# Chunk attention, gated projection and squared-ramp MLP on one core: heads swap rows by half block, weight combinations stored by pair into one tensor, a rounding step placed apart

## The chip, the cores and the metric

One core of one Trainium2 chip runs the whole program. The metric is the device time of one execution in microseconds (us); lower is better. All inputs and the output lie in the core's DRAM.

## The reference

Float64 inputs, q, k and v of 8 batches x 8 heads x 576 rows x 64, and five weight matrices. Attention works inside chunks of 64 rows; its output, 4608 tokens x 512, goes through a gated projection and then a second two-layer MLP. Cut to what matters:

```
scores = scale * matmul(q_c, k_c.T)            # per chunk of 64 rows, 9 chunks a head
attn = exp(scores - max); attn /= sum(attn) + 1e-9
x = matmul(attn, v_c)                          # (4608, 512) over the heads
x = (sigmoid(x @ w_gate) * (x @ w_val)) @ w_out        # d_ff 1536
h = x @ w2_in                                  # d_ff 2048
g = where(h >= 1, h, where(h <= -1, 0, (h + 1)**2 / 4))
out = g @ w2_out
```

q, k and v arrive as float32. The weights arrive as 8-byte floats, which the kernel itself turns into float32.

## The kernel before, in words

The program has four stages, one after the other.

**Stage 1** is attention and the gated projection, and it is the only one that the change touches. The 4608 tokens are cut into 9 blocks of 512 (`BS`), numbered 0 to 8. For each block, 24 projections (12 of w_gate, 12 of w_val, 12 matmuls each in `proj`: three products of high and low halves for each of 4 row groups) run on TensorE; ScalarE applies the sigmoid (L873), VectorE multiplies (L876), and the result is stored to DRAM (`g_store`, L760). One projection is one *slot*; a block is `NS` = 24 slots. Attention of block b is written into the slots of block b-1 (`later_block`), four head pairs `p` for each block: `load` brings q and k (L278), `v_load` brings v (L293), `t` transposes on VectorE (L304), `s` makes scores (L321), `m` and `e` subtract the maximum and take the exponential (L331 to L341), `n` and `w` normalise (L346 to L354), `p` and `c` transpose back (L360, L363), `o` multiplies with v (L373), `x` and `l` split the result into a high and a low half (L388, L392). Block 0's attention runs ahead of everything in `first_block`.

Because two 64-row heads share 128 partitions, the kernel gives the two heads turns at the upper and lower half: which head's chunk lies in which half of the rows flips ("trades") with every group `g` of 128 tokens, through the index `h ^ odd`. `v_load` therefore fetches v in pieces of at most two chunks, for each head apart.

In the same slots, from slot 26 on, the weights of the three later stages are made ready: `s_prep` takes a pair of weight tiles every 7 slots (22 pairs). It loads them (`w_load`), turns the 8-byte words into float32 (`w_low` and the VectorE half of `w_bits`, then a scaling on ScalarE, L124, then `w_join`), forms sums on GpSimd (`s_sums`), splits into high and low halves (`s_split`) and stores seven combinations (`s_spool`, L183) that the later stages load back (`s_load`, L187).

**Stages 2 to 4** (`down("o")`, `up`, `down("p")`) are matmuls with 7 products for 8 quarters, with operands from DRAM.

The order of the work is written out by hand: `at(slot, prio, fn, ...)` sorts the calls of a slot by fraction, priority and order of entry, and each engine does its share strictly in that order. All transfers are issued by SyncE (SP in the profile), one after the other. In the program's rows below, each transfer also waits for one of eight landing semaphores in turn (`DMAHW0` to `DMAHW7`), that is for the landing of the transfer eight before it.

Of the kernel before, what the change touches and what calls it, by code (L numbers as in the profile page):

```python
# [8 lines left out]
F32 = mybir.dt.float32  # L9
# [20 lines left out]
def kernel(  # L30
# [15 lines left out]
    nc = tc.nc  # L46
    P = 128
# [5 lines left out]
    CH = 64  # L53
    BS = 512
# [14 lines left out]
    dp = ctx.enter_context(tc.tile_pool(name="dp", bufs=1, space=bass.MemoryType.DRAM))  # L69
# [3 lines left out]
    uT = [dp.tile([F2 * P, GT], F32, name=f"uT{g}") for g in range(NG)]  # L73

    NWT = {"o": 7 * F1 // 4, "i": 7 * F2 // 4, "p": 7 * F2 // 4}
    sw = {
        kind: [dp.tile([P, 2, 2, 256], F32, name=f"sw{kind}{i}") for i in range(n)] for kind, n in NWT.items()
    }

    def f32(t):  # L80
        return t.bitcast(F32)
# [6 lines left out]
    keys = [(kind, f) for f in range(F1) for kind in "gv"]  # L88
    W = {}
    raws = {}  # L90
    stage = {}

    def words(raw):
        return lambda i, dt: raw.bitcast(dt).rearrange("p (n w) -> p n w", w=2)[:, :, i]
# [23 lines left out]
    def w_bits(key):  # L118
        word = words(raws[key])
        nc.vector.scalar_tensor_tensor(  # L120
            out=word(0, I32), in0=word(1, I32), scalar=-(2**31), in1=word(0, I32),
            op0=ALU.bitwise_and, op1=ALU.bitwise_or,
        )
        nc.scalar.activation(word(1, F32), word(1, F32), AF.Copy, scale=2.0**-112)  # L124

    def w_join(key):
# [28 lines left out]
    def s_place(kind, p, k):  # L155

        if kind == "i":
            return k // 2 * 7 + PO.index(p), k % 2
        return PO.index(p) * ((F1 if kind == "o" else F2) // 4) + k // 2, k % 2
# [18 lines left out]

    def s_spool(kind, k, part):
        products, st = stage.pop((kind, k, part))  # L180
        for i, p in enumerate(products):
            tile_, unit = s_place(kind, p, k)
            nc.sync.dma_start(out=sw[kind][tile_][:, unit], in_=f32(st[:, i]))  # L183

    def s_load(kind, i):
        w = wp.tile([P, 2, 2, 256], F32R, tag="w", name="w")
# [7 lines left out]
    def s_prep(kind, k):  # L194

        half_ = (F1 if kind == "o" else F2) // 2
        a, b = (kind, k), (kind, k + half_)
        return [
            (0, w_load, a), (0, w_load, b), (5, w_low, a), (5, w_bits, a), (6, w_low, b), (6, w_bits, b),
            (7, w_join, a), (7, w_join, b), (8, s_sums, kind, k), (9, s_split, kind, k, 0), (9, s_split, kind, k, 1),  # L200
            (10, s_split, kind, k, 2), (11, s_spool, kind, k, 0), (11, s_spool, kind, k, 1),
            (11, s_split, kind, k, 3), (12, s_spool, kind, k, 2), (13, s_spool, kind, k, 3),
        ]


# [3 lines left out]
    X = {}  # L209
# [24 lines left out]
    class Whole:  # L234
# [49 lines left out]
        def v_load(self, p):  # L284

            self.V[p] = t = self.alloc("vd").rearrange("p i (c e) -> p (i c) e", e=D)
            for off, m, bb, s0 in runs(self.b * BS, BS):
                c = off // CH
                while c < (off + m) // CH:
                    n = 2 - c % 2 if (off + m) // CH - c >= 2 else 1  # L290
                    for h in range(2):
                        at_ = s0 + c * CH - off
                        nc.sync.dma_start(  # L293
                            out=t[heads[h ^ c // 2 % 2], c:c + n],
                            in_=v[bb, 2 * p + h, at_:at_ + n * CH].rearrange("(c k) d -> k c d", k=CH),
                        )
                    c += n

        def t(self, p):
            qk, how, ident = self.qk[p], self.how[p], kv_["ident"]  # L300
# [25 lines left out]
        def m(self, p):  # L326
            s = self.SP[p][:, 0].rearrange("p (g h k) -> p g h k", h=2, k=CH)
            m = cp.tile([P, 2, NC], F32, tag="m0", name="m", bufs=2)
            banks = self.B.pop(("s", p))
            for h, b in enumerate(banks):  # L330
                nc.vector.tensor_reduce(out=m[:, h], in_=b, axis=AX.X, op=ALU.max)  # L331
            for h, b in enumerate(banks):
                for odd in range(2):
                    gs = slice(odd, NC, 2)
                    nc.vector.tensor_tensor(
                        out=s[:, gs, h ^ odd], in0=b[:, gs],
                        in1=m[:, h, gs].unsqueeze(2).to_broadcast([P, NC // 2, CH]), op=ALU.subtract,
                    )

# [25 lines left out]
        def o(self, p):  # L365

            banks = [self.bank(4 + r, [P, NC, 2, CH], "O") for r in range(2)]
            for g in range(0, NC, 2):
                for i in range(2):
                    for odd in range(2):  # L370
                        c = 2 * (g + odd) + i
                        for r, rows in enumerate(heads):
                            nc.tensor.matmul(  # L373
                                banks[r][heads[r ^ odd], g + odd, i],
                                lhsT=self.V[p][rows, c], rhs=self.SP[p][rows, 1, chunks[c]], start=True, stop=True,
                            )
            self.B["o", p] = banks

        def parts(self, p):
            for h, hs in enumerate(heads):  # L380
                for odd in range(2):
                    hi, lo = (X[self.b, p][hs, i].rearrange("p (g t) -> p g t", t=P)[:, odd::2] for i in range(2))
                    yield hi, lo, self.B["o", p][h ^ odd][hs, odd::2].rearrange("p g i t -> p g (i t)")

        def x(self, p):
            X[self.b, p] = x_tile()
# [7 lines left out]
    def first_block():  # L394
        ft = ps.tile([P, BS], F32, tag="b5", name="fill")

        def fill(n):
            for _ in range(n):
                nc.tensor.matmul(ft, lhsT=z[:, :P], rhs=z, start=True, stop=True)

        pieces = []
        for i in range(NW + 1):
            pieces.append((w_low, keys[i]))
            pieces.append((w_bits, keys[i]))
            if i:
                pieces.append((w_split, keys[i - 1]))
        nl = [0]

        def wl(n):
            for _ in range(n):  # L410
                w_load(keys[nl[0]])
                nl[0] += 1

        def conv(n):
            while n and pieces:
                fn, key = pieces.pop(0)
                fn(key)
                if fn is w_split and nl[0] < NW + 5:
                    wl(1)
                n -= fn is not w_low  # L420

        z = pool["sg"].tile([P, BS], F32R, tag="sg", name="z", bufs=4)
        nc.vector.memset(f32(z), 0.0)
        kv_["ident"] = cp.tile([P, P], F32, name="ident")
        make_identity(nc, kv_["ident"])
        a = Whole(
            0, [["b0", "b2", "b4"], "b1", "b3", "b6", "b7", "b5"],
            lambda nm: wp.tile([P, 2, BS], F32, tag="w", name=nm), "MVMT",
        )
        for c in LOADS:  # L430
            if c == "w":
                wl(1)
# [12 lines left out]
        conv(99)  # L445
        assert nl[0] == NW + 5, nl

# [39 lines left out]
    banks, B0, B1, OP, R_ = {}, {}, {}, {}, {}  # L487
# [280 lines left out]
    NW = 4  # L768
    for i, key in enumerate(keys):
        if i >= NW + 5:  # L770
            at(i - NW - 5, 2.5, w_load, key)
        if i > NW:
            at(i - NW - 1, 6, w_low, key)
            at(i - NW - 1, 6, w_bits, key)
        if i >= NW:
            at(i - NW, 5.5, w_split, key)
    slot = 26
    for kind, n in (("o", F1 // 2), ("i", F2 // 2), ("p", F2 // 2)):
        for pair in range(n):
            for dt, fn, *args in s_prep(kind, pair):  # L780
                at(slot + dt, 6 + dt / 10, fn, *args)
            slot += 7
# [11 lines left out]
    for i in range(FIRST):  # L794
        key, name = ("o", 0, i), ("o", 0, 1, i)
# [123 lines left out]
```

## Time and profile before

| | us |
|---|---|
| median of 3 runs | 1787.81 |
| the 3 runs | 1793.92, 1786.58, 1787.81 |
| the profiled execution | 1794.13 |
| its span in the trace | 1792.3 |
| its mean granted TensorE clock, share of full | 0.965 |

The trace gives busy time of the compute engines (PE is TensorE, PEld its weight load, DVE VectorE, ACT ScalarE, POOL GpSimd), waits with what ended them, the chain of work that ended last, and for SyncE the time in which each transfer was being issued (SPq) and when it landed. SyncE has no column of busy time; it is read from its timeline.

### The profile page before, as it was taken

Reading aid. Unit: us, or ns where it says so; the run is one execution under the profiler, and the core shown is the slowest. Engines: PE = TensorE matmul, PEld = TensorE weight load, DVE = VectorE, ACT = ScalarE, POOL = GpSimd, SP = SyncE. Lnnn points to the kernel's source line nnn. Section 1 sums busy time; section 2 is a strip of 40 time slices with the busy share of each in tenths; the row PEclk is TensorE's granted clock in tenths of the full one; section 3 lists DMA queues with packets and bytes.
Section 4 is the critical chain, followed back from the end, with each engine's and each line's share of the span. In section 5 each row is a group of like instructions: output and inputs, shape, how many; then the busy total and the mean of one; then the engine's idle time right before and its main releaser. Section 6 shows DMA issues by size and latency. Waiting matters only on the chain.

```text
span 1792.3 us, 30409 instructions
## 1 busy us (share of the span) xinstructions
PE 1677.1 (94%) x10658; PEld 1537.8 (86%) x10658; DVE 1193.9 (67%) x1874; ACT 870.0 (49%) x1632; POOL 833.7 (47%) x755
## 2 busy tenths in 40 slices
PE   6679987997889799999999999999999999999998
PEld 4567876776777678889999999999999989999998
DVE  5765544553545446217877787878887797889876
ACT  4554543443444255214555555555555445455453
POOL 2331442342334234106777775435442277677765
PEclk7889998998999899999999999999999999999999
DMA  6564565666666568683464465333234964644552
GB/s 159 142 174 114 161 199 171 169 195 177 180 180 199 170 168 241 219 302 106 154 223 142 142 235 223 142 147 144 106 142 182 360 228 123 169 143 105 133 150 36
DMA packets 392777, 307.19 MB, mean 171 GB/s; under 512 B 274992, under 2 KB 305712, under 8 KB 392624
## 3 DMA queue, kind: packets, MB, share of 16 engines
q1 hardware_dynamic: 392624, 305.24, 55.2%
q8 instruction: 84, 1.38, 0.3%
q14 instruction: 69, 0.57, 0.1%
HBM read 179.83 MB, written 125.30 MB: 170 GB/s over the span
## 4 chain that ended last, share of the span: by engine, by line
PE 63%; SPq 16%; DMA 9%; DVE 7%; issue 3%; ACT 1%; POOL 1%; DVEq 0%; ACTq 0%; POOLq 0%
PE P L471 16%; PE P L472 16%; PE P L470 16%; SPq L278 7%; SPq L293 5%; PE pr L470 5%; PE pr L471 4%; PE pr L472 4%; DMA gT<-sg 3%; DVE z L503 2%; DMA raw<-in_moe_w_gate_dram 2%; SPq L183 2%; DMA swi<-st 1%; DMA raw<-in_moe_w_out_dram 1%; DVE z L514 1%
## 5 line engine op out<-in xcount | busy, mean ns | idle before, releaser
L514 POOL TENSOR_TENSOR z<-z 128x384 fp32r<-128x384 f32 x305 | 356.3, 1190 | 308.7 <-ACT z L507 305.3
L471 PE MATMUL P<-z,w 128*128 128x384 f32 x1344 | 451.4, 336 | 4.9 <-POOL z L514 3.1
L470 PE MATMUL P<-z,w 128*128 128x384 f32 x1344 | 450.3, 335 | 0.0
L472 PE MATMUL P<-z,w 128*128 128x384 f32 x1344 | 450.1, 335 | 0.0
L470 PE MATMUL pr<-x,w 128*128 128x512 f32 x864 | 354.5, 410 | 0.0
L471 PE MATMUL pr<-x,w 128*128 128x512 f32 x864 | 345.7, 400 | 0.0
L472 PE MATMUL pr<-x,w 128*128 128x512 f32 x864 | 344.3, 399 | 0.0
L507 ACT ACTIVATE z<-z 128x384 fp32r<-128x384 f32 x420 | 205.8, 521 | 180.4 <-DVE z L503 106.8
L471 PEld LDWEIGHTS P<-z,w 128*128 128x128 f32 x1344 | 253.3, 188 | 7.5 <-POOL z L514 4.9
L514 POOL TENSOR_TENSOR op<-in,op 128x384 fp32r<-128x384 f32 x168 | 190.6, 1153 | 148.0 <-ACT op L507 147.2
L470 PEld LDWEIGHTS P<-z,w 128*128 128x128 f32 x1344 | 253.1, 188 | 0.4 <-ACT z L507 0.2
L472 PEld LDWEIGHTS P<-z,w 128*128 128x128 f32 x1344 | 253.4, 189 | 0.0
L876 DVE TENSOR_TENSOR sg<-pr,sg 128x512 f32<-128x512 f32 x108 | 74.5, 689 | 241.5 <-PE pr L472 112.0
L470 PEld LDWEIGHTS pr<-x,w 128*128 128x128 f32 x864 | 168.3, 195 | 37.0
L472 PEld LDWEIGHTS pr<-x,w 128*128 128x128 f32 x864 | 167.7, 194 | 37.1
L471 PEld LDWEIGHTS pr<-x,w 128*128 128x128 f32 x864 | 168.4, 195 | 33.8 <-DVE x L392 0.3
L507 ACT ACTIVATE op<-in 128x384 fp32r<-128x384 f32 x252 | 128.5, 523 | 112.8 <-PE P L472 59.1
L503 DVE TENSOR_TENSOR z<-z 128x384 f32<-128x384 f32 x200 | 172.4, 912 | 1.0 <-POOL z L514 0.9
L471 PE MATMUL P<-op,w 128*128 128x384 f32 x504 | 168.5, 334 | 0.1
L472 PE MATMUL P<-op,w 128*128 128x384 f32 x504 | 168.4, 334 | 0.0
L470 PE MATMUL P<-op,w 128*128 128x384 f32 x504 | 168.4, 334 | 0.0
L531 DVE TENSOR_TENSOR R<-P,R 128x384 f32<-128x384 f32 x216 | 115.7, 552 | 69.9 <-PE P L472 67.9
(63 smaller groups left out, 2208.9 us busy)
## 6 DMA issues: line engine op xcount, KB each, us to landing
uT<-ua SPq DMA_DIRECT2D x96, 384.0 KB, 2.4
z<-uT SPq DMA_DIRECT2D x96, 384.0 KB, 4.4
gT<-sg SPq DMA_DIRECT2D x108, 256.0 KB, 4.0
in<-gT SPq DMA_DIRECT2D x72, 256.0 KB, 3.7
raw<-in_moe_w_out_dram SPq DMA_DIRECT2D x28, 512.0 KB, 5.7
swi<-st SPq DMA_DIRECT2D x56, 256.0 KB, 3.0
swp<-st SPq DMA_DIRECT2D x56, 256.0 KB, 3.1
w<-swi SPq DMA_DIRECT2D x28, 512.0 KB, 6.4
```

The source lines that it names most:

```text
L183: nc.sync.dma_start(out=sw[kind][tile_][:, unit], in_=f32(st[:, i]))
L278: nc.sync.dma_start(out=t[32 * g:32 * g + 32, i, off // 32:(off + m) // 32], in_=rows[h, :, 32 * j:32 * j + 32].rearrange("(t i) r -> i t ...
L293: nc.sync.dma_start(out=t[heads[h ^ c // 2 % 2], c:c + n], in_=v[bb, 2 * p + h, at_:at_ + n * CH].rearrange("(c k) d -> k c d", k=CH),)
L470: nc.tensor.matmul(o, lhsT=ah, rhs=bh, start=first, stop=False, skip_group_check=open_)
L471: nc.tensor.matmul(o, lhsT=ah, rhs=bl, start=False, stop=False, skip_group_check=open_)
L472: nc.tensor.matmul(o, lhsT=al, rhs=bh, start=False, stop=last, skip_group_check=open_)
L503: (eng or nc.vector).tensor_tensor(out=op_src(p, key), in0=x, in1=y, op=ALU.subtract)
L507: nc.scalar.activation(o[:, 0], op_src(p, key), AF.Copy)
L514: eng.tensor_tensor(out=o[:, 1], in0=op_src(p, key), in1=f32(o[:, 0]), op=ALU.subtract)
L531: nc.vector.tensor_tensor(out=r(i), in0=b, in1=r(i), op=ALU.add)
L876: nc.vector.tensor_tensor(out=sg, in0=vo, in1=sg, op=ALU.mult)
```

## The change: what it does

Three edits, all in stage 1.

1. The heads trade rows once per block instead of with every 128 tokens: the first half of the block's groups has one order, the second half the other (`h ^ swap`). `v_load` then fetches up to four chunks in a transfer. `s`, `m`, `o`, `x` and `l` index by half instead of by odd and even; they issue as many instructions as before, and the four pieces of `x` and `l` become contiguous.
2. The combinations of one kind go into one DRAM tensor instead of one tensor for each tile, and `s_spool` stores both combinations of a staging tile by one transfer: four transfers for a weight pair instead of seven.
3. The ScalarE scaling is taken out of `w_bits` into `w_scale`. In `s_prep` VectorE's `w_low` and `w_bits` come one slot earlier (4 and 5 instead of 5 and 6), `w_scale` stays in slots 5 and 6, and the first `w_join` comes in slot 6 instead of 7. For the first stage's own weights the order is as before. The order on ScalarE and on GpSimd is unchanged, so that their rounding steps come later only against VectorE's.

```
-        kind: [dp.tile([P, 2, 2, 256], F32, name=f"sw{kind}{i}") for i in range(n)] for kind, n in NWT.items()
+    sw = {kind: dp.tile([n, P, 2, 2, 256], F32, name=f"sw{kind}") for kind, n in NWT.items()}
...
+    def w_scale(key):
+        word = words(raws[key])
         nc.scalar.activation(word(1, F32), word(1, F32), AF.Copy, scale=2.0**-112)
...
-        for i, p in enumerate(products):
-            tile_, unit = s_place(kind, p, k)
-            nc.sync.dma_start(out=sw[kind][tile_][:, unit], in_=f32(st[:, i]))
+        (a, unit), (b, _) = (s_place(kind, p, k) for p in (products[0], products[-1]))
+        nc.sync.dma_start(
+            out=sw[kind][a:b + 1:max(b - a, 1), :, unit].rearrange("n p h c -> p n h c"),
+            in_=f32(st[:, :len(products)]),
+        )
...
-            (0, w_load, a), (0, w_load, b), (5, w_low, a), (5, w_bits, a), (6, w_low, b), (6, w_bits, b),
-            (7, w_join, a), (7, w_join, b), (8, s_sums, kind, k), (9, s_split, kind, k, 0), (9, s_split, kind, k, 1),
+            (0, w_load, a), (0, w_load, b), (4, w_low, a), (4, w_bits, a), (5, w_scale, a), (5, w_low, b),
+            (5, w_bits, b), (6, w_scale, b), (6, w_join, a), (7, w_join, b), (8, s_sums, kind, k),
...
-                c = off // CH
-                while c < (off + m) // CH:
-                    n = 2 - c % 2 if (off + m) // CH - c >= 2 else 1
+                for swap in range(2):
+                    lo, hi = max(off, swap * half_), min(off + m, (swap + 1) * half_)
                     for h in range(2):
...
-                            out=t[heads[h ^ c // 2 % 2], c:c + n],
...
+                        if lo < hi:
...
+                                out=t[heads[h ^ swap], lo // CH:hi // CH],
...
-                for odd in range(2):
-                    gs = slice(odd, NC, 2)
+                for swap in range(2):
+                    gs = slice(swap * NC // 2, (swap + 1) * NC // 2)
```

What SyncE issues at the end of one head pair's v and for the first weight pair, early in stage 1 (the last four of the pair's v transfers, then the seven stores with the store of a projection between). Names: `vd` is v's tile, `swo_90` a DRAM tensor of the w_out combinations, `st` the staging tile, `gT` the stored projection; the shape is that of the destination, and the bracket is what the transfer waits for. Before:

```order
L293 DMA vd<-in_v_dram 64x2x64 [waits DMAHW2_49]
L293 DMA vd<-in_v_dram 64x2x64 [waits DMAHW3_49]
L293 DMA vd<-in_v_dram 64x2x64 [waits DMAHW4_49]
L293 DMA vd<-in_v_dram 64x2x64 [waits DMAHW5_49]
L183 DMA swo_90<-st 128x512 [waits DMAHW6_49,Pool_49]
L183 DMA swo_93<-st 128x512 [waits DMAHW7_49]
L183 DMA swo_99<-st 128x512 [waits DMAHW0_49,Pool_49]
L183 DMA swo_102<-st 128x512 [waits DMAHW1_49]
L760 DMA gT_67<-sg 128x512 [waits DMAHW2_49,DVE_49]
L183 DMA swo_96<-st 128x512 [waits DMAHW3_49,Pool_49]
L183 DMA swo_105<-st 128x512 [waits DMAHW4_49]
L183 DMA swo_87<-st 128x512 [waits DMAHW5_49,Pool_49]
```

The same place in the changed kernel:

```order
L297 DMA vd<-in_v_dram 64x2x64 [waits DMAHW2_49]
L297 DMA vd<-in_v_dram 64x2x64 [waits DMAHW3_49]
L297 DMA vd<-in_v_dram 64x4x64 [waits DMAHW4_49]
L297 DMA vd<-in_v_dram 64x4x64 [waits DMAHW5_49]
L183 DMA swo<-st 128x2x512 [waits DMAHW6_49,Pool_49]
L183 DMA swo<-st 128x2x512 [waits DMAHW7_49,Pool_49]
L766 DMA gT_67<-sg 128x512 [waits DMAHW0_49,DVE_49]
L183 DMA swo<-st 128x2x512 [waits DMAHW1_49,Pool_49]
L183 DMA swo<-st 128x512 [waits DMAHW2_49,Pool_49]
```

The head pair's eight v transfers became six here (four of two chunks, two of four), and seven stores became four; a store waits for the same engines as before. Over the program SyncE's rows fall from 1698 to 1504: 128 v transfers and 66 stores fewer, and no other transfer is added or moved past another.

VectorE at the first weight pair of `s_prep` (`raw` is the weight tile, L114 `w_low`, L120 `w_bits`, L128 `w_join`, `sg` the product of a projection), before:

```order
L304 STREAM_TRANSPOSE qkT<-qk 128x512 x2
L114 TENSOR_SCALAR raw<-raw 128x512
L120 SCALAR_TENSOR_TENSOR raw<-raw 128x512
L876 TENSOR_TENSOR sg<-pr,sg 128x512
L114 TENSOR_SCALAR raw<-raw 128x512
L120 SCALAR_TENSOR_TENSOR raw<-raw 128x512
L331 TENSOR_REDUCE m<-S 128x4 x2
L335 TENSOR_TENSOR sp<-S,m 128x2x64 x4
L128 SCALAR_TENSOR_TENSOR raw<-raw 128x512 x2
L876 TENSOR_TENSOR sg<-pr,sg 128x512
```

And in the changed kernel (L112, L118 and L129 are the same three steps):

```order
L307 STREAM_TRANSPOSE qkT<-qk 128x512 x2
L112 TENSOR_SCALAR raw<-raw 128x512
L118 SCALAR_TENSOR_TENSOR raw<-raw 128x512
L112 TENSOR_SCALAR raw<-raw 128x512
L118 SCALAR_TENSOR_TENSOR raw<-raw 128x512
L883 TENSOR_TENSOR sg<-pr,sg 128x512
L129 SCALAR_TENSOR_TENSOR raw<-raw 128x512
L334 TENSOR_REDUCE m<-S 128x4 x2
L338 TENSOR_TENSOR sp<-S,m 128x2x64 x4
L129 SCALAR_TENSOR_TENSOR raw<-raw 128x512
```

The second tile's two steps moved ahead of a projection's product, and the first join ahead of the maximum; the number of instructions is the same.

## Rows read from the trace of the kernel before

**Rows 1.** Windows: start to block 0, block 0, block 1, blocks 2 to 6, block 7, stages 2 to 4.
```profile
core 0: us, PE busy (x) PEld busy (x) DVE busy (x) ACT busy (x) POOL busy (x), PEclk, DMA share, GB/s
0.00:60.00 60.00, 31.57 (x397) 24.95 (x398) 30.61 (x78) 25.31 (x44) 11.84 (x15) 0.72 0.59 152
60.00:156.30 96.30, 81.03 (x560) 63.81 (x559) 70.65 (x136) 52.90 (x85) 32.16 (x24) 0.91 0.56 150
156.30:228.80 72.50, 72.50 (x561) 59.40 (x560) 39.57 (x89) 34.90 (x58) 21.68 (x23) 1.00 0.56 143
228.80:680.70 451.90, 391.47 (x2804) 316.35 (x2804) 219.59 (x464) 193.28 (x324) 152.63 (x159) 0.93 0.63 184
680.70:751.70 71.00, 71.00 (x523) 58.09 (x522) 32.32 (x71) 31.50 (x56) 22.50 (x23) 1.00 0.70 219
...
814.00:1793.00 979.00, 967.20 (x5546) 963.58 (x5544) 793.05 (x1025) 522.22 (x1050) 588.90 (x509) 1.00 0.50 161
```

**Rows 2.** Source line L873, 228.8 to 323.7: sigmoids of block 2, first and last start.
```profile
L873 ACT ACTIVATE sg<-pr x12: 570/598/602, 228.8 to 316.8; 128x512 f32<-128x512 f32 x12
```

**Rows 3.** Page, chain that ended last: shares of the span by line.
```profile
PE P L471 16%; PE P L472 16%; PE P L470 16%; SPq L278 7%; SPq L293 5%; PE pr L470 5%; PE pr L471 4%; PE pr L472 4%; DMA gT<-sg 3%; DVE z L503 2%; DMA raw<-in_moe_w_gate_dram 2%; SPq L183 2%; DMA swi<-st 1%; DMA raw<-in_moe_w_out_dram 1%; DVE z L514 1%
```

**Rows 4.** Waits, 228.8 to 680.7: total us, times, longest.
```profile
ACT st L172 <- DMA swi<-st: 45.8, 17, 8.9
...
DVE qkT L304 <- DMA qk<-in_k_dram: 41.7, 16, 3.9
...
DVE sg L876 <- ACT st L172: 32.9, 6, 6.3
DVE raw L114 <- DMA raw<-in_moe_w_in_dram: 22.0, 7, 8.2
...
DVE raw L114 <- DMA raw<-in_moe_w_out_dram: 15.2, 8, 5.1
```

**Rows 5.** Timeline of SP: start us, us, transfers issued back to back.
```profile
474.02 6.46 SPq L293 DMA_DIRECT2D vd<-in_v_dram  x10
480.58 0.54 SPq L183 DMA_DIRECT2D swi<-st  x1
481.16 1.05 SPq L105 DMA_DIRECT2D raw<-in_moe_w_in_dram  x2
```

**Rows 6.** Source lines L293 and L183, 228.8 to 680.7: issue ns min/median/max.
```profile
L293 SPq DMA_DIRECT2D vd<-in_v_dram x182: 465/605/2278, 238.0 to 668.5; - x182
...
L183 SPq DMA_DIRECT2D swi<-st x56: 375/562/1362, 362.4 to 549.4; - x56
L183 SPq DMA_DIRECT2D swo<-st x35: 376/597/1905, 230.4 to 343.7; - x35
L183 SPq DMA_DIRECT2D swp<-st x35: 371/529/2289, 568.4 to 679.1; - x35
```

**Rows 7.** Source lines L272 and L614, whole span: issue ns of nearest shapes.
```profile
L272 SPq DMA_DIRECT2D qk<-in_k_dram x2: 628/628/629, 18.5 to 19.2; - x2
...
L614 SPq DMA_DIRECT2D yT<-R x12: 371/371/371, 858.4 to 1077.3; - x12
```

**Rows 8.** Timelines of SP and PE at the start; bracket: idle before, releaser.
```profile
25.75 12.05 SPq L293 DMA_DIRECT2D vd<-in_v_dram  x16
...
40.68 8.89 SPq L278 DMA_DIRECT2D qk<-in_q_dram  x8
49.62 3.92 SPq L278 DMA_DIRECT2D qk<-in_k_dram  x8
...
56.34 0.92 PE L321 MATMUL S<-qkT 64*64 64x64 f32 x24 [11.92 <-DVE qkT L304]
```

**Rows 9.** DMA, 228.8 to 680.7: queue's share; KB each, median us to landing.
```profile
q1 hardware_dynamic: 149373, 82.56, 62.9%
...
raw<-in_moe_w_out_dram SPq DMA_DIRECT2D x20, 512.0 KB, 5.5
```

**Rows 10.** Source line L388, whole span: ns min/median/max, times, form.
```profile
L388 ACT ACTIVATE x<-O x144: 357/369/420, 25.1 to 742.3; 64x256 fp32r<-64x256 f32 x144
```

More of the change, by code (lines that the diff above doesn't have):

```diff
@@ L75 @@
     NWT = {"o": 7 * F1 // 4, "i": 7 * F2 // 4, "p": 7 * F2 // 4}
-    sw = {
-        kind: [dp.tile([P, 2, 2, 256], F32, name=f"sw{kind}{i}") for i in range(n)] for kind, n in NWT.items()
-    }
+    sw = {kind: dp.tile([n, P, 2, 2, 256], F32, name=f"sw{kind}") for kind, n in NWT.items()}
     def f32(t):
@@ L198, in s_prep @@
         return [
-            (0, w_load, a), (0, w_load, b), (5, w_low, a), (5, w_bits, a), (6, w_low, b), (6, w_bits, b),
-            (7, w_join, a), (7, w_join, b), (8, s_sums, kind, k), (9, s_split, kind, k, 0), (9, s_split, kind, k, 1),
-            (10, s_split, kind, k, 2), (11, s_spool, kind, k, 0), (11, s_spool, kind, k, 1),
-            (11, s_split, kind, k, 3), (12, s_spool, kind, k, 2), (13, s_spool, kind, k, 3),
+            (0, w_load, a), (0, w_load, b), (4, w_low, a), (4, w_bits, a), (5, w_scale, a), (5, w_low, b),
+            (5, w_bits, b), (6, w_scale, b), (6, w_join, a), (7, w_join, b), (8, s_sums, kind, k),
+            (9, s_split, kind, k, 0), (9, s_split, kind, k, 1), (10, s_split, kind, k, 2),
+            (11, s_spool, kind, k, 0), (11, s_spool, kind, k, 1), (11, s_split, kind, k, 3),
+            (12, s_spool, kind, k, 2), (13, s_spool, kind, k, 3),
         ]
@@ L286, in v_load @@
             self.V[p] = t = self.alloc("vd").rearrange("p i (c e) -> p (i c) e", e=D)
+            half_ = BS // 2
             for off, m, bb, s0 in runs(self.b * BS, BS):
-                c = off // CH
-                while c < (off + m) // CH:
-                    n = 2 - c % 2 if (off + m) // CH - c >= 2 else 1
+                for swap in range(2):
+                    lo, hi = max(off, swap * half_), min(off + m, (swap + 1) * half_)
                     for h in range(2):
-                        at_ = s0 + c * CH - off
-                        nc.sync.dma_start(
-                            out=t[heads[h ^ c // 2 % 2], c:c + n],
-                            in_=v[bb, 2 * p + h, at_:at_ + n * CH].rearrange("(c k) d -> k c d", k=CH),
-                        )
-                    c += n
+                        if lo < hi:
+                            nc.sync.dma_start(
+                                out=t[heads[h ^ swap], lo // CH:hi // CH],
+                                in_=v[bb, 2 * p + h, s0 + lo - off:s0 + hi - off].rearrange("(c k) d -> k c d", k=CH),
+                            )
         def t(self, p):
@@ L332, in m @@
             for h, b in enumerate(banks):
-                for odd in range(2):
-                    gs = slice(odd, NC, 2)
+                for swap in range(2):
+                    gs = slice(swap * NC // 2, (swap + 1) * NC // 2)
                     nc.vector.tensor_tensor(
-                        out=s[:, gs, h ^ odd], in0=b[:, gs],
+                        out=s[:, gs, h ^ swap], in0=b[:, gs],
                         in1=m[:, h, gs].unsqueeze(2).to_broadcast([P, NC // 2, CH]), op=ALU.subtract,
@@ L367, in o @@
             banks = [self.bank(4 + r, [P, NC, 2, CH], "O") for r in range(2)]
-            for g in range(0, NC, 2):
+            for g in range(NC // 2):
                 for i in range(2):
-                    for odd in range(2):
-                        c = 2 * (g + odd) + i
+                    for swap in range(2):
+                        g_ = g + swap * NC // 2
+                        c = 2 * g_ + i
                         for r, rows in enumerate(heads):
                             nc.tensor.matmul(
-                                banks[r][heads[r ^ odd], g + odd, i],
+                                banks[r][heads[r ^ swap], g_, i],
                                 lhsT=self.V[p][rows, c], rhs=self.SP[p][rows, 1, chunks[c]], start=True, stop=True,
@@ L380, in parts @@
             for h, hs in enumerate(heads):
-                for odd in range(2):
-                    hi, lo = (X[self.b, p][hs, i].rearrange("p (g t) -> p g t", t=P)[:, odd::2] for i in range(2))
-                    yield hi, lo, self.B["o", p][h ^ odd][hs, odd::2].rearrange("p g i t -> p g (i t)")
+                for swap in range(2):
+                    ts, gs = (slice(swap * n // 2, (swap + 1) * n // 2) for n in (BS, NC))
+                    hi, lo = (X[self.b, p][hs, i, ts] for i in range(2))
+                    yield hi, lo, self.B["o", p][h ^ swap][hs, gs].rearrange("p g i t -> p (g i t)")
         def x(self, p):
@@ L404, in first_block @@
             pieces.append((w_bits, keys[i]))
+            pieces.append((w_scale, keys[i]))
             if i:
@@ L419, in conv @@
                     wl(1)
-                n -= fn is not w_low
+                n -= fn not in (w_low, w_bits)
         z = pool["sg"].tile([P, BS], F32R, tag="sg", name="z", bufs=4)
@@ L774 @@
             at(i - NW - 1, 6, w_bits, key)
+            at(i - NW - 1, 6, w_scale, key)
         if i >= NW:
```

## Prediction, made before the changed kernel was run

> **What bounds the kernel now.** I read the windows first, cut where the first sigmoid of a block starts; a block has twelve of them [rows 1, 2]. Stages 2 to 4 keep TensorE busy 967 of 979 us at full clock [rows 1], and no edit is there: they stay. What can move is stage 1, the first 814 us. Two of its blocks show what TensorE alone needs for 24 projections and the next block's attention: block 1 took 72.5 us and block 7 took 71.0, both with TensorE busy throughout and a granted clock of 1.00, the 2.4 GHz level [rows 1]. I call 72 us the floor of a block. Against it block 0 took 96.3, and blocks 2 to 6 took 451.9 together, 90.4 each; there TensorE was busy 391 us and the mean granted clock was 0.93 [rows 1], so some of the time was at 1.2 GHz too. The excess is 24 us in block 0 and 92 in blocks 2 to 6, and in the first 60 us TensorE was busy only 32.
>
> What holds these blocks up? The chain of work names TensorE in the later stages, but apart from those its largest shares are issues on SyncE: q and k 7% of the span, v 5%, the stores of weight combinations 2%, together about 250 us [rows 3]. The waits say how that reaches the compute engines: in blocks 2 to 6 VectorE's transposes wait for k (41.7 us), `w_low` waits for raw weights (22.0 and 15.2), and ScalarE's split waits until a staging tile has been stored (45.8 for one of the three kinds), behind which the product `sg` waits on VectorE (32.9) [rows 4]. VectorE and ScalarE themselves are busy less than half of it [rows 1]. SyncE's timeline closes the argument: each issue starts as the one before ends, here ten v transfers in 6.46 us and the next at once [rows 5]. SyncE issues one transfer after another and is full; that is the bound of blocks 0 and 2 to 6. Block 1 needs fewer issues, since the weight pairs only start inside it.
>
> **The change part by part.** *Fewer v transfers.* A v issue takes a median 0.605 us [rows 6] and about 0.05 us passes before the next: ten take from 474.02 to 480.58, 0.656 each [rows 5]. A block's four pairs go from 40 (8 in a pair: 32) to 24 (where the block lies in one batch: 16). The v of blocks 3 to 7, loaded during blocks 2 to 6, goes by the code from 184 to 112 transfers (182 of them start inside the window [rows 6]): 72 x 0.655 = 47.2 us of SyncE saved. What remains has up to four runs a row; the nearest row is the k load with four runs of 256 B, 0.628 [rows 7], so at most 0.023 x 112 = 2.6 us come back, and at the least nothing. I take 2.6.
>
> *Fewer stores.* In the same stretch 126 stores took a median 0.56 (0.562, 0.597 and 0.529 by kind [rows 6]), 0.61 with the gap. Four for seven makes 72, so 54 x 0.61 = 33 us are saved. The issue of a store of two pieces is not in the trace: below, the two-run store of `yT` takes 0.371; above, the four-run load 0.628 [rows 7]. The stores here are already slower than the first, so I take 0.60: 72 x 0.04 = 3 us back. The net of both edits is 47 - 3 + 33 - 3, about 75 us (70 to 93 by those bounds). 451.9 - 75 = 377 us, 75 a block: SyncE then needs hardly more than TensorE's 72. I allow 1 us a block for waits that stay or meet at that balance: 380, that is **-72 us** in blocks 2 to 6. The ends are -92, the floor, and about -36, if half is lost.
>
> *Landing.* A transfer waits for the one eight before it. Where five weight loads stood ahead, eight q issues took 8.89 us, while the eight k behind them took 3.92 [rows 8]. A combined store carries 512 KB; a load of that size lands after 5.5 us [rows 9], longer than eight issues take. I leave SyncE's present waits in the 377 and add the 1 us; that they take back half of the gain is a rival.
>
> *Block 0.* Block 1's v is loaded in it, 40 transfers before and 24 after: 16 x 0.655 = 10.5 us. I take **-11**, with part of the next block's first v; the ends are 0 and -24.
>
> *Before block 0.* Block 0's own v falls from 32 to 16 transfers; the last sixteen alone take 12.05 us before five weight loads and block 1's q and k are issued, and TensorE then stands for 11.92 us until VectorE has transposed them [rows 8]. 16 transfers of 0.655 are 10.5 us: **-10**, with ends 0 and -12.
>
> *VectorE's earlier steps.* No instruction is added. A slot in blocks 2 to 6 is 451.9/120 = 3.8 us, so the first `w_low` of a pair asks for its load 3.8 us sooner. Queued behind it are the next product and the transposes, for which TensorE waits. If SyncE is on time the load is there: issue and landing, 5.5 us [rows 9], against four slots of 3 us. Then the cost is nothing, and ScalarE, whose scaling no longer meets its input just in time, may gain; I value both at 0. The bounds are -33 (the product's wait of 32.9 behind ScalarE [rows 4]) and +83 (22 pairs x 3.8).
>
> *The new order of rows.* `s`, `m`, `o`, `x` and `l` have as many instructions of as many elements. The profile prints the old pieces of `x` as 64x256, 0.369 us [rows 10], the shape they now have in one run. I take 0; 36 pairs hold 144 of each, so even 5% of that is 0.018 us each, 2.6 us on ScalarE, which is busy 43% of the stretch [rows 1].
>
> Blocks 1, 7 and 8 and the later stages: 0, since TensorE covers SyncE there. The sum is -10 - 11 - 72 = -93 against the profiled execution's 1794.1: 1701. That execution is 6 us above the median of the runs shown, 1787.8, and equals the slowest of them; against the median the sum would be 1695. I say **1700 us**.
>
> A row and a rule part here. By SyncE's rows an issue of 0.6 us with nothing between fills blocks 0 and 2 to 6 [rows 5, 6], and 194 issues fewer are worth the 93 us. The Trainium skill ("DMA: Bandwidth & Descriptors", section "Issuing engines are not separate DMA queues") says that issuing from several engines saves only sequencer time, "which is usually small relative to the DMA itself"; by that, saved issues would be worth nearly nothing. No run here has yet shown which; the rows speak for the sequencer, because many transfers are in flight at once and issues cannot overlap.
>
> **The rivals.**
> - *The floor.* SyncE falls behind TensorE everywhere, and with no gaps the clock stays at 2.4 GHz. For it: block 1 reached 72.5 [rows 1]. Against it: 75 is still above 72. -10 - 24 - 92 = -126: 1668.
> - *Given back by landings.* Half of the SyncE time saved turns into waits for the eight-back transfer. For it: 8.89 against 3.92 us [rows 8], and bigger stores. Against it: such waits are few now; the longest v issue is 2.278 us, but the median, 0.605, holds none [rows 6]. -93/2: 1748.
> - *No change.* Not the issues but the DMA engines bind. They are busy 62.9% in blocks 2 to 6 [rows 9] and move the same bytes in the same runs afterwards. Against it: they stood at 0.70 in block 7, which ran at its floor [rows 1]. 1788 to 1794. This is also where the page's rule would lead, by engines that set the pace whatever is issued.
> - *Slower: the early `w_low`.* If loads still come more than four slots after they are due, each first `w_low` stands up to 3.8 us longer, and the product and the transposes behind it: up to +83. With half of the SyncE gain, -46, it makes +37: 1831. It decides from the point where SyncE's lag exceeds four slots less the 5.5 us of landing, about 9.5 us. For it: the 37 us that `w_low` waits already [rows 4]. Against it: those are 15 waits, and the lag shrinks.
>
> **How the numbers follow.** Near balance, 1680 to 1725: 0.55. The floor: 0.15. Half given back: 0.19. No change: 0.05. Slower: 0.06. A measurement of this kernel can tell about 0.5%, 9 us, from no change. The first three are faster: 0.89; a little of the last two cases may still be faster, so 0.90, same 0.04, slower 0.06. The range goes from just above the floor to just below the half, 1672 to 1742: it holds the 0.55, most of the floor's chance and about half of the half's, 0.8 together.
>
> **What would show it.** Right: SP's timeline has 112 v issues of about 0.63 us and 72 stores of about 0.6 in blocks 2 to 6, and holes between them; those blocks take 73 to 78 us each at a clock near 1.00; VectorE's waits for k and raw weights fall below a third; TensorE's stop of 11.92 us before block 0 falls under 3. Wrong: stores that take over 1 us to issue; waits of SyncE for landings that grow past 70 us; blocks 2 to 6 still near 90 us though SP has holes (another bound); or `w_low` waiting longer than its 37 us.

## The result and the profile after

The changed kernel takes 1725.99 us (median of 4 runs, 1722.68 to 1728.4) against 1789.74 us for the kernel before in the same comparison: a ratio of 0.9641, 95% interval 0.9613 to 0.9669, about 64 us less. The forecast was 1700 us with a range of 1672 to 1742. The profiled executions differ a little more, 1720.9 against 1792.3 us of span, because that of before was its slowest run and that of after its fastest.

The windows of the changed kernel, cut at the same points of the program as [rows 1]: up to block 0, block 0, block 1, blocks 2 to 6, block 7, and stages 2 to 4.

```profile
core 0: us, PE busy (x) PEld busy (x) DVE busy (x) ACT busy (x) POOL busy (x), PEclk, DMA share, GB/s
0.00:52.80 52.80, 31.27 (x405) 25.14 (x406) 30.82 (x78) 25.47 (x43) 11.86 (x15) 0.81 0.69 175
52.80:142.30 89.50, 78.76 (x552) 61.73 (x551) 69.86 (x137) 53.34 (x86) 32.50 (x24) 0.92 0.60 160
142.30:214.80 72.50, 72.50 (x561) 59.39 (x560) 40.68 (x90) 34.38 (x58) 22.98 (x24) 1.00 0.61 163
214.80:609.90 395.10, 371.90 (x2801) 301.86 (x2801) 215.48 (x462) 194.37 (x325) 151.93 (x157) 0.97 0.73 208
609.90:681.50 71.60, 71.60 (x526) 58.57 (x525) 32.54 (x71) 31.32 (x56) 22.54 (x23) 1.00 0.67 208
...
743.80:1721.00 977.20, 965.91 (x5545) 960.24 (x5543) 793.70 (x1025) 521.55 (x1050) 588.66 (x509) 1.00 0.49 162
```

The time left where it was forecast: 7.2 us before block 0, 6.8 in block 0, 56.8 in blocks 2 to 6 (451.9 to 395.1), and nothing in blocks 1 and 7; the later stages differ by 2. The compute engines do the same work (VectorE 215 us against 220). But blocks 2 to 6 are not at the floor of 5 x 72. Apart, they show where:

```profile
214.80:296.20 81.40, 75.44 (x561) 61.17 (x561) 42.72 (x90) 39.45 (x66) 31.87 (x32) 0.96 0.72 204
296.20:368.70 72.50, 72.50 (x561) 59.38 (x560) 43.19 (x94) 38.59 (x64) 27.19 (x28) 1.00 0.74 209
368.70:451.70 83.00, 75.57 (x563) 61.28 (x563) 43.22 (x92) 38.82 (x65) 31.91 (x34) 0.96 0.70 205
451.70:526.80 75.10, 72.62 (x559) 58.80 (x558) 42.86 (x92) 39.20 (x66) 29.73 (x30) 1.00 0.74 209
526.80:609.90 83.10, 75.78 (x561) 61.23 (x560) 43.50 (x94) 38.30 (x65) 31.24 (x33) 0.96 0.75 214
```

Blocks 3 and 5 are at it or near; blocks 2, 4 and 6 stay nine to eleven us above. SyncE's queue is still full: the gaps of more than 0.15 us between its issues add up to 18 of the 395 us, against 12 of 452 before. SyncE's own lines in blocks 2 to 6 (issue ns, min/median/max), which answer to [rows 6], show the new v transfers and stores, and what they cost:

```profile
L297 SPq DMA_DIRECT2D vd<-in_v_dram x112: 489/622/1348, 218.0 to 609.4; - x112
...
L183 SPq DMA_DIRECT2D swi<-st x32: 378/620/1346, 325.3 to 491.3; - x32
L183 SPq DMA_DIRECT2D swp<-st x20: 373/544/1172, 509.7 to 604.9; - x20
L183 SPq DMA_DIRECT2D swo<-st x17: 382/702/1216, 214.4 to 309.7; - x17
```

A v issue takes 0.622 us at the median, as estimated. A store takes longer than a small one did in all three kinds (0.620, 0.544 and 0.702 us at the median, against 0.562, 0.529 and 0.597). Summed from the trace's rows, the 68 stores whose issues are recorded there take 47.6 us and the 126 of before took 75.6.

### The profile page after: what moved, and what is told of

Read it like the earlier page. It is cut to its first block, busy times and chain, and to the rows that moved or that the text cites. A ratio compares the mean times of both kernels' runs of the same rounds, so it can differ in the third digit from the quotient of the medians.

```text
span 1720.9 us, 30155 instructions
## 1 busy us (share of the span) xinstructions
PE 1654.2 (96%) x10658; PEld 1518.5 (88%) x10658; DVE 1191.2 (69%) x1874; ACT 870.3 (51%) x1632; POOL 834.5 (48%) x755
## 4 chain that ended last, share of the span: by engine, by line
PE 75%; SPq 8%; DVE 6%; DMA 6%; issue 2%; POOL 2%; ACT 1%; DVEq 0%; POOLq 0%; ACTq 0%
PE P L477 17%; PE P L478 17%; PE P L476 17%; PE pr L476 8%; PE pr L477 7%; PE pr L478 7%; SPq L282 5%; DVE z L509 2%; SPq L297 2%; DMA gT<-sg 1%; DMA raw<-in_moe_w_gate_dram 1%; PE O L377 1%; DVE z L520 1%; PE S L324 1%; DMA raw<-in_moe_w_in_dram 1%
## 5 line engine op out<-in xcount | busy, mean ns | idle before, releaser
L476 PE MATMUL P<-z,w 128*128 128x384 f32 x1344 | 449.5, 334 | 0.2 <-DVE R L537 0.2
L476 PE MATMUL pr<-x,w 128*128 128x512 f32 x864 | 349.0, 404 | 0.0
L477 PE MATMUL pr<-x,w 128*128 128x512 f32 x864 | 341.4, 395 | 0.3 <-DVE x L397 0.3
L478 PE MATMUL pr<-x,w 128*128 128x512 f32 x864 | 341.4, 395 | 0.0
L478 PEld LDWEIGHTS pr<-x,w 128*128 128x128 f32 x864 | 165.0, 191 | 35.9
L476 PEld LDWEIGHTS pr<-x,w 128*128 128x128 f32 x864 | 165.3, 191 | 35.4
L477 PEld LDWEIGHTS pr<-x,w 128*128 128x128 f32 x864 | 165.4, 191 | 33.5 <-DVE x L397 0.7
L880 ACT ACTIVATE sg<-pr 128x512 f32<-128x512 f32 x108 | 64.5, 597 | 221.8 <-PE pr L478 212.0
```

The lines of the kernel that those rows point to most:

```text
L476: nc.tensor.matmul(o, lhsT=ah, rhs=bh, start=first, stop=False, skip_group_check=open_)
L477: nc.tensor.matmul(o, lhsT=ah, rhs=bl, start=False, stop=False, skip_group_check=open_)
L478: nc.tensor.matmul(o, lhsT=al, rhs=bh, start=False, stop=last, skip_group_check=open_)
L880: nc.scalar.activation(sg, go, AF.Sigmoid)
```

## The experiments

All twelve runs were timed against the kernel before, whose median lay between 1789.1 and 1790.5 us in those comparisons. The ratios are to that.

### Which edit carries the gain

**Edits 1 and 2 without edit 3**: the changed kernel with `s_prep`'s old slots.

```
-            (0, w_load, a), (0, w_load, b), (4, w_low, a), (4, w_bits, a), (5, w_scale, a), (5, w_low, b),
-            (5, w_bits, b), (6, w_scale, b), (6, w_join, a), (7, w_join, b), (8, s_sums, kind, k),
+            (0, w_load, a), (0, w_load, b), (5, w_low, a), (5, w_bits, a), (5, w_scale, a), (6, w_low, b),
+            (6, w_bits, b), (6, w_scale, b), (7, w_join, a), (7, w_join, b), (8, s_sums, kind, k),
```

> The change without its third edit: VectorE's two steps and the first join stand in their old slots, rows and stores as changed. Theory A (SyncE's issues bound stage 1 and the earlier VectorE steps run into loads that are not there yet: w_low waits 60.6 us for raw weights in the changed kernel): about 1715 us, 10 below the changed kernel's 1726, and w_low's waits for raw weights fall under 35 us in blocks 2 to 6. Theory B (the prediction's own value, the order is worth nothing): 1726. Theory C (the new order helps ScalarE and so part of the gain is its own): 1732 to 1740.

Measured: 1724.22 us, ratio 0.963 (0.9612 to 0.9648). Theory A of the third edit falls, and so does C; B, that the order is worth nothing, holds. The waits moved as A said: the changed kernel's VectorE waits for raw weights grew from 37 us [rows 4] to 60.6, here first the changed kernel's and then this run's rows for blocks 2 to 6.

```profile
DVE raw L112 <- DMA raw<-in_moe_w_out_dram: 36.4, 8, 9.5
...
DVE raw L112 <- DMA raw<-in_moe_w_in_dram: 24.2, 8, 10.1
```

```profile
DVE sg L883 <- ACT st L173: 41.6, 10, 5.7
...
DVE raw L112 <- DMA raw<-in_moe_w_in_dram: 17.4, 7, 4.6
...
DVE raw L112 <- DMA raw<-in_moe_w_out_dram: 11.1, 7, 2.9
```

With the old slots they are 28.5, but the product then waits longer behind ScalarE (41.6 us against 24.7 in the changed kernel). A shorter wait at one place came back at the next; the time did not move.

**Edit 1 alone** (rows by half block, fewer v transfers, on the kernel before; the diff is that of the front part from `v_load` on).

> The kernel before with the first edit alone (heads trade rows by half block, fewer v transfers). Theory A: 128 issues of some 0.65 us fewer, 10 before block 0, 10 in block 0, 45 in blocks 2 to 6 on SyncE, of which some seven tenths arrive as they did for the whole change: 1789 - 45, about 1744. Theory D (the DMA engines and not the issues set the pace): within 5 us of 1789, since the bytes and runs are the same.

Measured: 1725.54 us, 0.9635 (0.9617 to 0.9653). Edit 1 alone gives the whole gain, about 64 us, more than the 45 expected; theory D falls. Its window of blocks 2 to 6:

```profile
210.40:610.90 400.50, 375.33 (x2804) 304.51 (x2803) 219.62 (x464) 193.35 (x325) 152.38 (x159) 0.97 0.71 205
```

**Edit 2 alone** (one tensor a kind, four stores a pair).

> The kernel before with the second edit alone (one tensor a kind, four stores a pair). Theory A: 54 issues fewer in blocks 2 to 6, 30 us of SyncE, seven tenths of it: about 1768. Theory D: within 5 us of 1789. Against A would also be a larger gain than the first edit's.

Measured: 1787.15 us, 0.9985 (0.9972 to 0.9998): some 2 to 3 us. Theory A's number fails. SyncE does issue 54 fewer stores in blocks 2 to 6, but each takes longer in two of the three kinds (the window, then issue ns again):

```profile
230.40:675.80 445.40, 386.04 (x2805) 311.87 (x2804) 219.53 (x464) 193.22 (x325) 152.25 (x159) 0.94 0.65 186
```

```profile
L180 SPq DMA_DIRECT2D swi<-st x32: 378/702/2106, 364.1 to 547.1; - x32
L180 SPq DMA_DIRECT2D swo<-st x20: 376/752/1163, 232.5 to 345.2; - x20
L180 SPq DMA_DIRECT2D swp<-st x20: 366/502/1168, 567.7 to 673.3; - x20
```

Summed from the trace, the stores' issues fall from 75.6 us (126) to 53.3 (72), 22 us, and not by the 30 of the forecast's net; and the other issues of the stretch, in the same or nearly the same numbers, lengthen by 15.5: v by 4.4, raw weights by 3.4, gT by 6.0, q and k by 1.7. The net of 7 is about what the blocks lost, 451.9 to 445.4. Part of that is scatter between executions: two runs described below whose edits changed no time, edit 3 alone and the order of rows alone, had 449.5 and 448.6 there.

What lengthens the issues can be read at one place of the queue, the same in the program's order. A few large transfers stand there (three stores of `gT`, the stores of the combinations and two loads of raw weights), and behind them 26 small ones of v, q and k. First the kernel before, then this run, then the run with longer stores that comes further down; in each pair the large ones are first.

```profile
411.83:419.33 7.50, 5.21 (x44) 4.31 (x45) 3.94 (x10) 1.35 (x2) 3.94 (x5) 0.58 0.94 324
419.33:435.04 15.71, 14.32 (x65) 11.48 (x64) 6.30 (x12) 7.24 (x12) 4.59 (x5) 1.00 0.54 130
```

```profile
411.90:419.64 7.74, 5.44 (x42) 4.42 (x43) 3.94 (x10) 1.37 (x2) 4.16 (x6) 0.57 0.93 318
419.64:435.39 15.75, 14.86 (x67) 11.93 (x65) 6.30 (x12) 7.25 (x12) 4.31 (x4) 0.99 0.53 127
```

```profile
437.94:449.06 11.12, 8.84 (x57) 7.16 (x58) 3.94 (x10) 3.59 (x8) 5.41 (x6) 0.69 0.96 359
449.06:465.30 16.24, 11.45 (x53) 9.15 (x51) 6.52 (x12) 5.13 (x7) 3.11 (x3) 0.93 0.52 127
```

Before, twelve large transfers take 7.50 us; here nine with the same bytes, 2.4 MB, take 7.74; with longer stores twelve with 4.0 MB take 11.12. The time follows the bytes and not the number, and the DMA engines' share is 0.93 to 0.96 there. During the small transfers it is 0.52 to 0.54. The share of 0.63 over the whole stretch hides this.

The rest of blocks 2 to 6 fits, reckoned from the trace's packets: 79 issues of this run took over 0.9 us, and in the half microsecond before them the DMA engines were busy to 0.92 on average, against 0.53 before the other issues. The long issues are no waits for the landing of the transfer eight before. Such a wait stands ahead of an issue and not in it: for each of the 711 issues of the kernel before in this stretch, that transfer had landed when the issue started. And the time between issues adds up to 51.7 us here and was 51.5 before. How nearly full DMA engines lengthen an issue on SyncE is not shown by any run.

**Edit 3 alone.**

> The kernel before with the third edit alone (VectorE's steps one slot earlier, scaling apart). Theory A: SyncE is as late as before, so the earlier w_low waits longer: 1800 to 1815. Theory B: 1789. Theory C: 1775 to 1785.

Measured: 1791.31 us, 0.9999 (0.9985 to 1.0014). Nothing, as theory B has it; A's loss and C's gain both fail.

### Is it the number of v transfers, and is it SyncE?

**The new order of rows with the old number of v transfers** (edit 1 with v again in pieces of two chunks):

```
...
-                        if lo < hi:
-                            nc.sync.dma_start(
-                                out=t[heads[h ^ swap], lo // CH:hi // CH],
...
+                    c = lo // CH
+                    while c < hi // CH:
+                        n = min(2 - c % 2, hi // CH - c)
+                        for h in range(2):
+                            nc.sync.dma_start(out=t[heads[h ^ swap], c:c + n], ...
```

> The kernel before with the new order of rows (heads trade by half block), but v still fetched in as many transfers of at most two chunks as before. If the fewer v issues carry the first edit's gain (theory A), this stays at the kernel before: 1784 to 1794. If the order of rows itself carries it (matmuls, VectorE and ScalarE reading by half instead of by odd and even), it takes about 1726, as the first edit alone did.

Measured: 1791.25 us, 1.0004 (0.9992 to 1.0017). The order of rows is worth nothing by itself; the fewer transfers carry the gain.

**v of blocks 1 to 8 issued by ScalarE**, on the kernel before, same transfers:

```
-                        nc.sync.dma_start(
+                        (nc.scalar if self.b else nc.sync).dma_start(
```

> The kernel before with v of blocks 1 to 8 issued by ScalarE instead of SyncE, in as many transfers; the eight landing semaphores stay shared between both queues. If SyncE's issue time alone binds, 256 issues leave it: blocks 0 and 2 to 6 fall to the floor of 72 us, 1690 to 1710, unless ScalarE's own order stalls. If the window of eight transfers binds (a new transfer waits for the landing of the one eight before it), little is won: 1760 to 1800, and ScalarE's issues wait for landings.

Measured: 1817.03 us, 1.0149 (1.0124 to 1.0174), slower, and beyond both expectations. In this run the two queues take turns at the same eight landing semaphores, so a transfer of SyncE waits for a v transfer that ScalarE issues late; SyncE's queue waits of stage 1 show it, and below them a wait of ScalarE:

```profile
SPq L278 <- DMA vd<-in_v_dram: 83.5, 53, 6.9
SPq L183 <- DMA vd<-in_v_dram: 19.3, 4, 7.1
SPq L109 <- DMA vd<-in_v_dram: 13.9, 3, 5.1
```

```profile
ACT sg L873 <- DMA vd<-in_v_dram: 107.9, 20, 8.4
```

So ScalarE's sigmoid came after v transfers (107.9 us in 20 waits), which the product and TensorE then waited for. Issue time on SyncE fell (from 400.7 to 256.1 us in blocks 2 to 6) and nothing was won. Whether the shared landings or ScalarE's own delay did it, this run does not settle.

**v of blocks 1 to 8 issued by GpSimd**, the same line with `nc.gpsimd`:

> The kernel before with v of blocks 1 to 8 issued by GpSimd, whose transfers have eight landing semaphores of their own, in as many transfers. If SyncE binds, by issues or by its window of eight: 1690 to 1720, since both are freed. If the DMA engines bind: within 10 us of 1789, since bytes and runs are the same. If issuing on GpSimd costs over 1 us each, GpSimd's sums and normalising come late: 1730 to 1780.

Measured: 1701.44 us, 0.9515 (0.9497 to 0.9533). Window of blocks 2 to 6:

```profile
223.00:588.90 365.90, 364.36 (x2804) 297.00 (x2803) 222.57 (x464) 191.42 (x324) 256.98 (x341) 1.00 0.76 223
```

With the bytes, runs and number of transfers of the kernel before, all five blocks lie at the floor, 73.2 us each, at 2.4 GHz throughout, and the DMA engines are at 0.76. So neither the DMA engines' whole load nor any compute engine held these blocks up at 90 us; SyncE's one queue did, in which small transfers at a low share of the DMA engines and large ones at a high share stand one behind the other. With v on a queue of its own the gaps of more than 0.15 us in SyncE's add up to 63 of the 366 us.

**The seven small stores issued by GpSimd**, v left on SyncE:

```
-            nc.sync.dma_start(out=sw[kind][tile_][:, unit], in_=f32(st[:, i]))
+            nc.gpsimd.dma_start(out=sw[kind][tile_][:, unit], in_=f32(st[:, i]))
```

> The kernel before with the seven small stores of each weight pair issued by GpSimd, which has just made the last half of the staging tile. SyncE loses 154 issues of 0.6 us and their places in its window of eight: by theory A about 14 us a block in blocks 2 to 6, so 1725 to 1745; combining them (1787) freed only issues, and the longer landings gave most of it back. If the stores never were on the path that binds: 1784 to 1794, as combining them did.

Measured: 1755.0 us, 0.9807 (0.9793 to 0.9822). Taking the stores off SyncE gives 35 us, ten less than the nearer end of the expectation, where combining them gave 2 to 3: the stores are on the queue that binds, and combining them hardly shortened it. Blocks 2 to 6:

```profile
230.70:642.50 411.80, 380.94 (x2801) 307.67 (x2801) 223.91 (x464) 191.78 (x325) 216.34 (x279) 0.96 0.67 197
```

The 75.6 us of store issues left SyncE there, but its other issues, nearly as many as before, grew from 325 to 354 us (v from 118 to 135, q and k from 154 to 170). The stores' bytes still move beside them; that this is why they grew fits the rows above and is not shown.

**As many stores, six in seven of them twice as long**, on SyncE; the added half goes to spare DRAM that is not read:

```
...
-            nc.sync.dma_start(out=sw[kind][tile_][:, unit], in_=f32(st[:, i]))
+            n = len(products)
+            nc.sync.dma_start(out=sw[kind][tile_][:, unit, :n], in_=f32(st[:, :n]))
...
```

> The kernel before with as many stores as before, but each of six in seven carries its staging tile whole (512 KB instead of 256), the other half going to spare DRAM that is never read. Issues are unchanged; landings and bytes grow. If SyncE's window of eight makes landings count (what I now think took back the gain of combining the stores), it is slower: 1805 to 1830, with SyncE's v issues of blocks 2 to 6 growing longer. If only the number of issues counts: 1785 to 1796.

Measured: 1857.81 us, 1.0376 (1.035 to 1.0402), 67 us slower, 28 beyond the far end of the expectation; 58.6 of it stand in blocks 2 to 6, whose window follows with the stores' issues (line L185 here) and their landings.

```profile
230.80:741.30 510.50, 405.63 (x2810) 327.44 (x2810) 221.28 (x465) 193.52 (x324) 153.29 (x159) 0.89 0.70 217
```

```profile
L185 SPq DMA_DIRECT2D swi<-st x56: 375/984/1452, 382.3 to 595.6; - x56
L185 SPq DMA_DIRECT2D swo<-st x35: 375/1017/1553, 233.9 to 362.7; - x35
L185 SPq DMA_DIRECT2D swp<-st x35: 320/771/1411, 615.2 to 740.0; - x35
...
DMA to landing us min/median/max: 2.6/5.0/8.8
```

As many issues, but the stores hold SyncE for 0.77 to 1.02 us at the median instead of 0.53 to 0.60, and land after 5.0 us instead of 3.1. Of the 58.6 us, 32 are the stores' issues (75.6 to 107.9), 15 the other issues, of which v has only 4, and 12 the time between issues, where waits for landings stand. So the sign that was expected, longer v issues, hardly came. Nor does a store issue slowly because it is itself long: the 18 that stayed at 256 KB took 0.99 us on average, the 108 of 512 KB 0.84, and the 126 of before 0.60. The mean share of the DMA engines, 0.70, is below the 0.76 at which the run with v on GpSimd had its floor, but where the stores stand it is 0.96, as the rows shown with edit 2 have it. The price of the stores on this queue therefore follows the bytes that they bring, while their number stayed.

### Versions that go on from there

**Edit 1 and v of blocks 1 to 8 on GpSimd:**

> The kernel before with the first edit, and v of blocks 1 to 8 issued by GpSimd. Neither edit 2 nor edit 3. If SyncE with its window is the one bound of stage 1, both gains meet at the floor: blocks 2 to 6 at 73 us each (365), the start and block 0 as in the first edit alone: 1685 to 1695. If GpSimd's issues cost stage 1 something, 1700 or more.

Measured: 1691.89 us, 0.945 (0.9423 to 0.9476), 34 us below the changed kernel and the fastest of all. Its first stretches show where stage 1 still stands off its floor:

```profile
0.00:52.30 52.30, 30.13 (x397) 24.16 (x398) 30.80 (x78) 25.25 (x44) 12.76 (x17) 0.69 0.72 177
52.30:142.80 90.50, 78.18 (x559) 61.77 (x559) 73.97 (x136) 53.54 (x84) 53.44 (x59) 0.95 0.58 161
215.30:582.50 367.20, 364.62 (x2805) 296.93 (x2804) 222.51 (x464) 191.32 (x324) 217.75 (x269) 1.00 0.76 222
```

**The same with the seven stores on GpSimd too:**

> As the run with v on GpSimd and the first edit, but the seven stores of each weight pair go from GpSimd too. At the floor nothing is left to win in blocks 2 to 6: 1685 to 1697. If GpSimd becomes the late one (its waits for landings stand before its sums and normalising): 1700 to 1730.

Measured: 1695.35 us, 0.9471 (0.9449 to 0.9494). Nothing more, as expected near a floor.

**Edit 1 with the seven stores on GpSimd, v on SyncE:**

> The first edit with the seven stores issued by GpSimd and v by SyncE. If the stores' places on SyncE are what keeps the changed kernel above the floor in blocks 2, 4 and 6: 1690 to 1702. If they are not: about 1726, as with the first edit alone.

Measured: 1696.99 us, 0.9483 (0.9446 to 0.9521). Blocks 2 to 6:

```profile
212.00:585.80 373.80, 367.40 (x2804) 298.81 (x2803) 224.03 (x464) 191.55 (x324) 216.67 (x278) 0.99 0.74 217
```

Four of the five are at 72.5 to 73.7 us; block 5 still takes 81.4. So the stores' places on SyncE are most of what keeps edit 1 alone above the floor (400.5 to 373.8), and, by inference, the changed kernel, which takes the same time with its stores combined.

## Why the prediction was right, and where its sum was off

**The bound.** Right. That SyncE's queue, and not the DMA engines, VectorE or ScalarE, held blocks 2 to 6 at 90 us was argued from its gapless timeline and is now shown: the same transfers spread over two queues bring those blocks to 73.2 us. What the prediction had wrong is that the queue is full of issues at a fixed price everywhere. For v, q and k that nearly held; where the stores stand the DMA engines are busy to 0.93 and more, and the rival that they bind, dismissed by a mean of 62.9%, is right there.

On the row and the rule the measurement decides: the Trainium skill ("DMA: Bandwidth & Descriptors", section "Issuing engines are not separate DMA queues") calls the sequencer time that spreading DMAs over engines saves usually small. In this kernel, where some 140 transfers stand in one queue for each block, moving 288 of them to GpSimd is worth about 89 us. The same section says that the transfers of all issuing engines run on the same 16 DMA engines; in that run no cost of it shows, at a share of 0.76.

**Fewer v transfers.** The step is right, and nearly in size: -47 + 3 in blocks 2 to 6, -10 and -11 ahead of them make about -65, and edit 1 alone measured -64. Its parts differ: blocks 2 to 6 gave 51 (451.9 to 400.5), the first two stretches less than written in the changed kernel (-7.2 and -6.8). TensorE's stop of 11.92 us before block 0 [rows 8] fell to 2.70, as forecast:

```profile
48.80 0.58 PE L324 MATMUL S<-qkT 64*64 64x64 f32 x24 [2.70 <-DVE qkT L307]
```

**Fewer stores.** This is the term that failed: "the net of both edits is 47 - 3 + 33 - 3" priced a combined store at 0.60 us and the rest of the queue at its old price (its bounds, added up again, are 73 to 94, not 70 to 93). It was worth 2 to 3 us alone and nothing measurable beside edit 1, instead of 30. It counted a store's price by the number of issues; what the runs show is that the price follows the bytes, which combining leaves as they are. Nine large transfers took 7.74 us where twelve with the same bytes had taken 7.50, at a share of 0.94 of the DMA engines; more bytes in as many transfers cost 67 us. The rival "given back by landings" comes near in effect, for the stores alone and nearly whole instead of half of everything, but not in its cause: the time between SyncE's issues, where a wait for the transfer eight before would stand, did not grow (51.5 and 51.7 us). The prediction looked for such waits inside the issues (the 2.278 us of the longest v issue); the trace has them ahead of the issues. In the run with longer stores it grew by 12 of 58.6. Several of the expectations rest on that window of eight; for the stores the traces speak against it, and for v on ScalarE the waits shown speak for it. Stores taken off SyncE are worth 35 us.

**The number.** 1726 us lies in the range, but just past the 1680 to 1725 of "near balance", which had 0.55. Of the forecast's 93 us the v terms came, about 65 written and 64 measured, and the stores' 30 did not; the range was wide enough to hold a number with one whole term missing, and in that the total had luck.

**The balance.** "75 a block" assumed that both savings arrive; with one, blocks 2, 4 and 6, which load eight raw tiles and issue 14 to 16 stores where blocks 3 and 5 have six and 11 or 12, stayed SyncE's at 81 to 83 us, and blocks 3 and 5 came to 72.5 and 75.1. The holes that SyncE's timeline was to have, as a sign of being right, did not appear either (18 us of 395).

**VectorE's earlier steps.** Valued at 0, and they are worth 0 in both surroundings. One of the signs given for a wrong prediction did appear, `w_low` waiting 60.6 us instead of 37, and it cost nothing that the time shows. The check "below a third" for VectorE's waits failed also for k (41.7 to 19.1).

**The new order of rows.** Valued at 0; 1.0004 with the old number of transfers.

**The rivals.** No change, and slower through `w_low`, are excluded by the interval. The floor was not reached by the change, but the runs with v on GpSimd reached it in blocks 2 to 6, or nearly (366 to 370 us).

Left open: block 0 takes 89.5 us in the changed kernel and 90.5 in the best version, with v off SyncE; what holds it 18 us above the floor was not tried. VectorE is busy 74.0 of those 90.5 us, which makes it the first to look at.

## What to carry to other kernels

When an engine that only issues transfers shows no gap in its timeline, count its queue like a compute engine, but look at the share of the DMA engines at each place of the queue and not only at its mean. Where the share was low here, the number of transfers was the price: many small transfers made half as many gave all they cost. Where it was near 1, the bytes were: joining two large stores into one gave almost nothing. What helped both was a second queue with landing semaphores of its own on an engine with time to spare. The one tried on ScalarE, which shared them, made the kernel slower, for a reason that is not settled. A wait that grows in the trace is not yet a loss: two of them traded places here with no change of time.

## What was not expected of the hardware

- An issue on SyncE can take several times its least without a wait that the profile shows. A store's took from 0.32 us to 1.55 in the run with longer stores, and its own size did not decide (0.99 us on average at 256 KB, 0.84 at 512 KB). Long issues went with a high share of the DMA engines: in the half microsecond ahead of the 121 issues of over 0.9 us in that run's blocks 2 to 6 it was 0.97 on average, ahead of the others 0.52.
- GpSimd's issues are no dearer than SyncE's here: 288 v transfers took a median of 0.602 us, against 0.605 on SyncE, and the stores 0.542 with hardly any spread, as the rows of the two runs show. But they are work of GpSimd (its busy time in blocks 2 to 6 rose from 152.6 to 257.0 us with v), and the stores landed later, after 5.5 us at the median instead of 3.1.

```profile
L293 POOL DMA_DIRECT2D vd<-in_v_dram x288: 523/602/772, 58.5 to 624.6; - x144
```

```profile
L183 POOL DMA_DIRECT2D swi<-st x56: 539/542/767, 326.6 to 501.2; - x56
```

- In the run with v on GpSimd the DMA engines carried 223 GB/s at a share of 0.76 in blocks 2 to 6 with TensorE busy 364.4 of 365.9 us, although 83192 of their 130917 packets were of 128 bytes (10.6 of 81.5 MB).
